# A new order for the first two fifths of a one-core adaLN, linear-attention and gated-MLP kernel

## The chip, the cores and the metric

The kernel runs on one core of a Trainium2 chip. The core has five engines that run side by side: TensorE (PE in the profile, with its weight loads as PEld), VectorE (DVE), ScalarE (ACT), GpSimd (POOL) and SyncE (SP), which here issues nearly all DMAs. Each engine works through its own list of instructions in order; semaphores hold an instruction until what it needs is there. The metric is the device time of one launch in microseconds, as the median of several runs.

## The reference

All data is bfloat16. `x` has 2048 rows of 512, there are 32 heads of 16, and the MLP has 1376 hidden columns.

```
mod = (silu(c) @ w_mod) as six rows sa, ca, ga, sb, cb, gb of 512
h   = layernorm(x) * (1 + ca) + sa
q, k, v = split(h @ wqkv)                      # 32 heads of 16
pq, pk  = q @ w_phi, k @ w_phi                 # per head, 16 x 16
phi_q   = concat(softmax(pq), softmax(-pq));  phi_k likewise
kv, z   = sum over s of phi_k (x) v,  sum over s of phi_k
o   = (phi_q @ kv) / (phi_q @ z + 1e-6)
x   = x + ga * (o @ wo)
h   = layernorm(x) * (1 + cb) + sb
x   = x + gb * ((sigmoid(h @ w_gate) * (h @ w_up)) @ w_down)
```

## The kernel before

The 2048 rows are 16 tiles of 128, called t0 to t15. The kernel is one flat program of 1230 tasks. A function builds each task with a name, the engines that may run it, what it reads and writes, and the buffers that it uses. The text `ORDER` at the head of the file then lists all task names once. `Graph.arrange` reads it from left to right: the position in the text sets the order of the tasks on each engine, and also which buffer slot a task's result gets, since slots are handed out in this order from a queue of free ones. A name without a suffix runs on the first engine in its list; `@A`, `@D` or `@P` put it on ACT, DVE or POOL. There are eight PSUM banks, seven slots of 2 KB for exponentials and features, and a few small ones. Nothing else orders the work; the kernel's estimates of task lengths are not used when it runs.

The tasks that matter here, in the order in which one tile passes through them:

- `ld_...` on SP: loads. `ld_x0b` brings tiles 2 and 3, `ld_wk0` a half of the key weights, `ld_wm00a` to `ld_wm01b` quarters of the modulation weights for the first norm.
- `warm0` (six matmuls) and `warm1_0` to `warm1_11` (one matmul each) on PE compute nothing that is used. They multiply zeros so that TensorE's clock comes up and stays up.
- `st1_t` (DVE, lines 702 and 703): mean and variance of tile t. `rs1_g` (ACT lines 709 and 710, or POOL lines 712 and 713): the reciprocal root for a group g of one or two tiles. Groups 0 and 1 are tiles 0 and 1, group 2 is tiles 2 and 3, and so on. `nmr1_g` (DVE, line 718): minus mean times this root. `xn1_t` (POOL line 731, ACT line 727; DVE line 729 for tile 0): the normalized tile.
- `tphgj` (PE, line 744): transposes of column block j of a group. For groups 6 and 7 a DMA does it (`xT1_t`, line 736). `hm1_gj` (DVE, ACT or POOL, lines 751 and 753): scale and shift by the modulation, into `h1T`.
- `modc1.0` and `modc1.1` (PE, line 630) with `modc1c0` and `modc1c1` make the modulation for column blocks 0 and 1, and for 2 and 3.
- `tpwk`, `wTck`, `fold1j`, `foldc1j` (PE and ACT in turn, lines 661, 664, 679, 685): `w_phi` is multiplied into the key weights, so that keys come out as `pk`. `fold0j` does it for the queries. `bd` (POOL, line 580) arranges `w_phi` as a block matrix for it.
- `Kt` (`Kta`, `Ktb` where split), `Vt`, `Qt` (PE, lines 817, 821, 871): the projections. `et` (ACT, line 776): exponentials of plus and minus `pk`. `nt` (DVE, line 780): their sums per head. `rt` (DVE line 798, or ACT lines 794 and 795): the reciprocals. `phit` (DVE or POOL, line 787): the key features. `vat` (ACT, line 836): the values with a column of ones, which `pmem` (POOL, lines 586 and 587) has written. `kvt` (PE, line 282): the sums over rows, into two PSUM banks. A number behind a dot says which eighth of the heads a split task begins with.
- `qet`, `qnt`, `qphit.s` (ACT line 776, DVE line 780, POOL or DVE line 784): the same for queries. `pTt` (SP): a DMA transposes the query features.
- `kvz0`, `kvn0`, `kvz1`, `kvn1` (DVE, lines 299 and 294) copy the finished sums out, and `num0a` (PE, line 326) is the first numerator. Then come `rd`, `u`, `oT`, `out`, `x1`, the second norm (`st2`, `rs2`, `nmr2`, `xn2`), and the MLP (`g`, `tg`, `u`, `hm`, `y`, `fin`).

Of the kernel before, what the change touches and what calls it, by code (L numbers as in the profile page):

```python
# [1058 lines left out]
```

## Time and profile before

| what | us |
|---|---|
| runs shown | 202.90, 204.34, 409.55 |
| their median | 204.34 |
| the profiled execution, its own time | 203.25 |
| its span, from the first to the last instruction | 201.3 |
| first numerator on PE | 56.47 |

The third run took twice as long as the others and is not used. In the rows of the profile the first two numbers are the start and the length in microseconds; a number in square brackets is the idle time of the engine before the row, with what ended it. An instruction's row often reaches about 0.1 us over the start of the next one on its engine, so what an instruction costs is best read from start to start. A row with x2 or more merges neighbours of one line and form. Row lengths of PE include the time that a result takes to come out; the pace of a row of matmuls is the distance of their starts.

### The profile page before, as it was taken

To read this page: it belongs to the slowest core of one execution; us is meant where nothing else is said; L and a number is where in the kernel's file an instruction comes from. 1 tells how busy PE (TensorE), PEld (TensorE's weight loads), DVE (VectorE), ACT (ScalarE), POOL (GpSimd) and SP (SyncE) were. 2 spreads that over 40 slices of the span, in tenths; PEclk is the share of its full clock that TensorE was granted. 3 is DMA by queue.
4 is the path that set the end of the run, shared out by engine and by line. 5 is a ranking of instruction groups with operands and counts; after the bars stand their busy time and mean duration, and the time that the engine had idled before them with its cause. 6 is when DMAs were issued, how large, how long until landed. Compare 5 with 4: busy or idle time off the path is not lost.

```text
span 201.3 us, 4128 instructions
## 1 busy us (share of the span) xinstructions
PE 193.6 (96%) x1447; PEld 106.1 (53%) x1471; DVE 160.0 (79%) x376; ACT 104.9 (52%) x250; POOL 103.9 (52%) x146
## 2 busy tenths in 40 slices
PE   7889999999999999999999999999999999999993
PEld 2555665455565777668744444444444444444442
DVE  3999999999999999997997796875969662326632
ACT  2899999999978974486621215312112420334100
POOL 4889978887899998876660166130030332000000
PEclk9999999999999999999999999999999999999999
DMA  5999956729964883455573334442113031000011
GB/s 163 336 292 236 295 204 126 113 62 268 396 248 78 133 111 68 85 34 105 104 80 80 70 62 102 84 110 56 25 25 74 2 78 55 26 8 26 28 55 55
DMA packets 49453, 22.94 MB, mean 114 GB/s; under 512 B 38065, under 2 KB 47634, under 8 KB 49426
## 3 DMA queue, kind: packets, MB, share of 16 engines
q1 hardware_dynamic: 48896, 22.59, 48.8%
q8 instruction: 13, 0.21, 0.4%
q14 instruction: 14, 0.11, 0.2%
q10 hardware_dynamic: 530, 0.02, 0.1%
HBM read 11.58 MB, written 2.10 MB: 68 GB/s over the span
## 4 chain that ended last, share of the span: by engine, by line
PE 64%; DVE 26%; issue 5%; ACT 2%; DMA 1%; DVEq 0%
PE y_ps L485 19%; PE u_ps L447 18%; PE g_ps L447 18%; DVE ks L780 6%; PE a_ps L356 5%; DVE st L702 5%; DVE qks L780 3%; DVE phi L787 3%; DVE kr L798 2%; PE num L326 2%; DVE h1T L753 2%; DMA x_sb<-in_A_x_dram 1%; DVE mv L703 1%; PE g_ps L449 1%; DVE nmr L718 1%
## 5 line engine op out<-in xcount | busy, mean ns | idle before, releaser
L457 ACT ACTIVATE tg<-g_ps 128x512 bf16<-128x512 f32 (+5 forms) x66 | 28.7, 455 | 66.6 <-PE g_ps L447 39.7
L468 DVE SCALAR_TENSOR_TENSOR wmod_sb<-tg,u_ps 128x512 bf16<-128x512 bf16 (+4 forms) x63 | 30.2, 491 | 18.1 <-ACT tg L457 11.5
L485 PE MATMUL y_ps<-wd_sb,wmod_sb 128*128 128x512 bf16 (+4 forms) x180 | 44.2, 366 | 0.2
L447 PEld LDWEIGHTS <-wg_sb 128*128 128x128 bf16 (+1 forms) x252 | 21.9, 99 | 16.1 <-issue 0.2
L447 PEld LDWEIGHTS <-wu_sb 128*128 128x128 bf16 (+1 forms) x252 | 21.7, 99 | 15.9 <-issue 0.2
L784 POOL TENSOR_TENSOR qphi<-qe,qks 128x512 bf16<-128x512 bf16 x24 | 25.2, 1066 | 3.9 <-DMA pT<-qphi 1.6
L485 PEld LDWEIGHTS <-wmod_sb 128*128 128x128 bf16 (+1 forms) x187 | 17.1, 98 | 16.0 <-issue 0.6
L447 PE MATMUL u_ps<-wT_sb,wu_sb 128*128 128x512 bf16 (+2 forms) x124 | 23.8, 322 | 0.1
L447 PE MATMUL g_ps<-wT_sb,wg_sb 128*128 128x512 bf16 (+2 forms) x122 | 23.0, 321 | 0.2
L447 PE MATMUL g_ps<-wqk_sb,wg_sb 128*128 128x128 bf16 (+4 forms) x127 | 19.9, 286 | 0.1
L447 PE MATMUL u_ps<-wqk_sb,wu_sb 128*128 128x128 bf16 (+4 forms) x127 | 19.8, 286 | 0.1
L492 DVE TENSOR_TENSOR ot<-y_ps,x 128x512 bf16<-128x512 f32 (+2 forms) x17 | 11.1, 654 | 10.4 <-PE y_ps L485 10.3
L780 DVE TENSOR_REDUCE ks<-e 128x64 f32<-128x1024 bf16 (+2 forms) x22 | 19.2, 901 | 0.0
L780 DVE TENSOR_REDUCE qks<-qe 128x64 bf16<-128x1024 bf16 x16 | 19.1, 1202 | 0.0
L376 POOL TENSOR_SCALAR ve<-mv 128x2 f32<-128x2 f32 (+1 forms) x8 | 1.8, 225 | 33.3 <-DVE mv L366 33.2
L776 ACT ACTIVATE e<-k_ps 128x512 bf16<-128x512 f32 (+2 forms) x44 | 18.2, 519 | 0.0
L776 ACT ACTIVATE qe<-q_ps 128x512 bf16<-128x512 f32 x32 | 17.0, 611 | 0.8 <-POOL phi L787 0.5
L817 PE MATMUL k_ps<-wqk_f,h1T 128*128 128x512 bf16 x61 | 16.0, 379 | 0.1
L787 POOL TENSOR_TENSOR phi<-e,kr 128x1024 bf16<-128x1024 bf16 (+2 forms) x10 | 14.8, 1484 | 2.6 <-DVE phi L787 1.2
L356 PE MATMUL a_ps<-wo_sb,oT 128*128 128x512 bf16 x60 | 15.9, 379 | 0.2
L871 PE MATMUL q_ps<-wqk_f,h1T 128*128 128x512 bf16 x61 | 15.7, 379 | 0.1
L821 PE MATMUL v_ps<-wv_sb,h1T 128*128 128x512 bf16 x61 | 15.4, 379 | 0.1
(132 smaller groups left out, 305.6 us busy)
## 6 DMA issues: line engine op xcount, KB each, us to landing
out_dram<-ot SPq DMA_DIRECT2D x15, 128.0 KB, 1.7
x_sb<-in_A_x_dram SPq DMA_DIRECT2D x6, 256.0 KB, 4.7
wmod_sb<-in_w_mod_dram SPq DMA_DIRECT2D x1, 1536.0 KB, 7.0
wu_sb<-in_B_w_up_dram SPq DMA_DIRECT2D x1, 1376.0 KB, 11.5
wg_sb<-in_B_w_gate_dram SPq DMA_DIRECT2D x1, 1376.0 KB, 11.9
wd_sb<-in_B_w_down_dram SPq DMA_DIRECT2D x1, 1280.0 KB, 8.5
wmod_sb<-in_w_mod_dram SPq DMA_DIRECT2D x4, 256.0 KB, 6.1
wqk_sb<-in_A_wqkv_dram SPq DMA_DIRECT2D x2, 256.0 KB, 4.4
```

The lines of the kernel that those rows point to most:

```text
L356: pe.matmul(ap_[:], lhsT=oT[:, j, :], rhs=wo_sb[:, j, :], start=(j == 0), stop=(j == KT - 1))
L447: pe.matmul(ps[:fsz, 0:n], lhsT=w[:, j, ft * P:ft * P + fsz], rhs=h[:, j, 0:n], start=(j == 0), stop=(j == KT - 1))
L457: G.add(f"tg{k}.{ft}", {"ACT": 0.13 + n * 0.00083}, lambda e, tg=tg, g_ps=g_ps, fsz=fsz, n=n: act.activation(tg[:fsz, 0:n], g_ps[:fsz, 0:n ...
L468: dve.scalar_tensor_tensor(hm_all[:fsz, hm[k].slot, ft, 0:n], tg[:fsz, 0:n], 1.0, u_ps[:fsz, 0:n], op0=ALU.add, op1=ALU.mult)
L485: mm = pe.matmul(y[:, 0:c1 - c0], lhsT=hm_all[:fsz, hm[k].slot, ft, tl * P:(tl + 1) * P], rhs=wd_sb[:fsz, ft, c0:c1], start=(ft == 0), sto ...
L776: act.activation(ee[:, a:b, s].rearrange("p g f h -> p g (f h)"), kp[:, a * 64:b * 64].rearrange("p (g n) -> p g n", n=64), ACT.Exp, scale ...
L780: dve.tensor_reduce(ks[:, a:b].rearrange("p g s h -> p (g s) h"), ee[:, a:b].rearrange("p g s f h -> p (g s) h f"), axis=AX.X, op=ALU.add)
L784: engine(e).tensor_tensor(ph[:].rearrange("p (g s f h) -> p g s f h", s=2, f=DH, h=4)[:, :, s], ee[:, :, s], ks[:, :, 1 - s].unsqueeze(2). ...
L787: engine(e).tensor_tensor(ph[:, a * P:b * P].rearrange("p (g f h) -> p g f h", f=DH, h=4), ee[:, a:b].rearrange("p g s f h -> p (g s) f h" ...
L817: pe.matmul(kp[:], lhsT=h1T[:, j, t * P:(t + 1) * P], rhs=wqk_f[:, j, D:2 * D], start=(j == 0), stop=(j == KT - 1))
L821: pe.matmul(vp[:], lhsT=h1T[:, j, t * P:(t + 1) * P], rhs=wv_sb[:, j, :], start=(j == 0), stop=(j == KT - 1))
L871: pe.matmul(qp[:], lhsT=h1T[:, j, t * P:(t + 1) * P], rhs=wqk_f[:, j, 0:D], start=(j == 0), stop=(j == KT - 1))
```

## The change

The first 405 names of `ORDER`, up to the copies of `wo` before the first numerators, stand in a new order. From there on the text is the same. Three tasks change engine: `xn1_3` from ACT to POOL, `rs1_0` from POOL to ACT, and `qphi2.0` from DVE to POOL. Besides this,

- on PE, five warm-ups instead of eight stand ahead of the first transposes of the key weights (`tpw1`, `tpw0`), and the others are spread out; tile 1 goes ahead of tiles 3, 0 and 2 in the key projections;
- on POOL, `pmem` moves from ahead of `bd` to behind `xn1_3` and `xn1_2`;
- on DVE, the statistics and the scale-and-shift tasks change places, `hm1_10` comes after `nmr1_4` and `st1_11` instead of before, and the sums of the keys run in the order 3, 0, 1, 2 instead of 0, 2, 3, 1;
- on ACT, `foldc13` comes ahead of the `hm1` tasks, and the exponentials run in the order 1, 3, 0, 2 instead of 0, 2, 3, 1;
- on SP, only `wmod_free`, which issues nothing, changes places with `ld_wu0`.

Which slot of a bank or buffer a task gets follows the new text too.

```diff
--- before.py
+++ after.py
@@ -37,25 +37,25 @@
 SPLIT = {"wk": 2, "wv": 1, "wq": 2, "wg": 1, "wu": 1, "x1": 2, "x2": 2, "x3": 1}
 LETTER = {"A": "ACT", "D": "DVE", "P": "POOL"}
 ORDER = """
-wdz warm0 c1 warm1_0 warm1_1 warm1_2 warm1_3 warm1_4 warm1_5 warm1_6 warm1_7 ld_x0b pmem ld_x0a ld_wk0 tpw1 tpw0 bd c2 mask4 st1_3 st1_2 st1_1 ld_x1b warm1_8
-rs1_2 rs1_1 nmr1_2 ld_wk1 xn1_3@A c3 wTc1 ld_x1a warm1_9 xn1_2 tph22 tph20 tpw2 tph21 wTc0 nmr1_1 st1_6 wTc2 xn1_1 tph13 ld_wm00b st1_0 tph10 tpw3 wTc3 fold10
-rs1_0@P fold12 st1_7 foldc10 ld_wm00a foldc12 fold11 modc1.0 rs1_4@P ld_x2b warm1_10 foldc11 modc1c0 st1_5 tph11 tph12 ld_wm01b warm1_11 st1_4 rs1_3@P
-hm1_20@A xn1_0 hm1_10 hm1_11@A hm1_21@A tph01 tph23 fold13 tph00 nmr1_4 xn1_6 xn1_7 ld_wm01a st1_11 hm1_01@A foldc13 st1_10 modc1.1 K3a modc1c1@D ld_x2a
-hm1_00@A tph02 hm1_23 rs1_6@P hm1_13@A hm1_02 nmr1_3 st1_9 st1_8 xn1_5 tph03 K0a tph41 hm1_03@A tph40 xn1_4 K2a hm1_22@A hm1_12@A hm1_41@A hm1_40 wqT1 nmr1_6
-ld_x3a st1_15 fold01 foldc01 tph42 K2b hm1_42@A K0b K3b e0.0 ld_wv0 tph32 tph30 tph31 wqT3 tph33 rs1_5@P nmr1_5 K1a hm1_32 xn1_11 hm1_30@A st1_14 n0.0 st1_12
-xn1_10 xn1_9 K1b e2.0 e3.0 rs1_8@P V0a wqT2 xn1_8 hm1_31@A tph43 V2a V2b nmr1_8 xn1_15 xn1_14 ld_wmga wqT0 V3a V3b va3 V0b fold03 V1a modca.0 modca.1 hm1_33
-tph50 V1b e1.0 K5a n2.0 r0.0@A modcac hm1_50 n3.0 hm1_43@A foldc03 xT1_11 fold02 fold00 foldc02 phi0.0 tph52 foldc00 xT1_10 va2 va1 n1.0 va0 K5b K4a r3.0
-st1_13 tph53 hm1_63@P hm1_60@P K4b hm1_62@P Q0 hm1_53@A tph51 Q1 ld_wmm2 tph82 hm1_51@A r2.0@A Q2 r1.0 phi3.0@D phi1.0@D hm1_82@A qe0.0 Q4 modc2.0 phi2.0@D
-rs1_7@P nmr1_7 xn1_12 hm1_52 qe2.0 ld_wo xn1_13 kv0.0 kv1.0 kv2.0 tph83 kv3.0 qe1.0 qn0.0 xT1_12 e5.0 modc2.1 xT1_13 modc2c K6a K6b qphi0.0@P e4.0 qn2.0
-qphi0.1@P tph80 qn1.0 pT0 hm1_80@A qphi2.1 qphi2.0 pT2 K7a K7b qe4.0 n4.0 V6 va6 r4.0@A n5.0 V5 va5 tph81 V4 qn4.0 phi4.0@D qphi1.1@P r5.0@A va4 qphi1.0@P
-hm1_70@P K9 K8 hm1_61@P qphi4.0@P kv4.0 pT1 phi5.0 hm1_72@P qphi4.1 e6.0 hm1_83 hm1_81 V9 n6.0 V7 pT4 hm1_71 e9.0 e7.0 va7 K11 n9.0 e8.0 e11.6 e11.0 r6.0
-r9.0@A ld_wd2 n7.0 kv5.0 r7.0@A e11.2 gwa K14 V8 e14.0 phi6.0 e14.4 e11.4 n8.0 n11.6 phi7.0@D n11.0 K10 n14.0 n11.2 r8.0 r11.0 va9 kv6.0 hm1_73@P e10.0 gra
-va8 K12 phi9.0 kv7.0 K15 n11.4 r11.2 V10 phi8.0 V11 n14.4 r14.0 r11.6 gwb e12.0 va10 K13 kv8.0 phi11.6 kv9.0 Q6 ld_wd r11.4 n10.0 r14.4@A wmod_free V14 V13
-phi11.4@D va11 n12.0 r10.0@A phi11.0@D phi11.2@D e13.4 phi10.0@D e13.0 e15.4 kv10.0 e15.0 kv11.4 kv11.6 ld_wu0 kv11.0 kv11.2 n13.4 va13 grb V12 Q3 wo1 phi14.0
-r12.0@A phi14.4 V15 qe6.0 va12 n13.0 r13.4 phi13.4 n15.0 r13.0 n15.4 r15.4@A phi15.4 r15.0 va14 phi13.0@D phi15.0@D Q5 phi12.0@D ld_wg0 kv12.0 kv13.0 va15
-kv14.0 qn6.0 wo0 wo3 kv15.0 kvz0 kvn0 kv13.4 kv14.4 kv15.4 kvz1 kvn1 num0a num1a num2a wo2 rd0a wo_all rd1a qe3.0 u0a num0b num4a num1b rd0b Q11 qe5.0 rd2a
-u0b u2a rd4a num2b qn3.0 u1a rd1b tpo0 Q8 qphi6.0@P qphi6.1@P oT0 out0 num4b rd2b u1b wd0 qe11.0 u2b qphi3.1@P qphi3.0@P x1_0 rd4b st2_0 qe8.0 Q7 qe7.0 tpo1
-oT1 Q10 Q9 out1 Q15 oT2 rs2_0 qn5.0 nmr2_0 xn2_0 u4a u4b x1_1 qn7.0 tsw xnT0 out2 qphi5.1@P qphi5.0@P pT6 mod02 mod00 qphi7.0@P pT3 mod03@A mod01@A qe15.0
+ld_x0b wdz warm0 c1 bd mask4 c2 ld_x0a ld_wk0 warm1_0 st1_3 warm1_1 warm1_2 st1_2 warm1_3 warm1_4 rs1_2 tpw1 st1_1 rs1_1 tpw0 ld_x1b nmr1_2 ld_wk1 wTc1
+warm1_5 warm1_6 fold11 wTc0 st1_0 rs1_0 warm1_7 tpw3 xn1_3 xn1_2 tph22 ld_x1a fold10 c3 nmr1_1 st1_7 pmem st1_6 tph21 st1_5 tpw2 warm1_8 foldc11 wTc3 ld_wm00b
+ld_wm00a xn1_1 tph10 wTc2 tph11 fold13 ld_x2b st1_4 warm1_9 fold12 foldc10 modc1.0 xn1_0 ld_wm01b foldc13 rs1_4@P nmr1_4 warm1_10 ld_wm01a warm1_11 foldc12
+tph23 rs1_3@P tph00 xn1_7 modc1c0 hm1_11@A tph02 tph01 hm1_00@A st1_11 tph20 tph13 hm1_10 hm1_01@A tph12 hm1_21@A st1_10 modc1.1 modc1c1@D ld_x2a nmr1_3
+hm1_20@A xn1_6 wqT1 K1a hm1_12@A rs1_6@P tph03 hm1_02 K3a hm1_03@A hm1_23 hm1_22@A tph41 xn1_5 st1_8 fold01 hm1_13@A tph43 hm1_43@A hm1_41@A K2a foldc01 st1_9
+tph40 K2b xn1_4 K1b nmr1_6 K0a ld_x3a hm1_40 tph30 rs1_5@P tph32 tph33 tph31 e1.0 st1_15 hm1_33 ld_wv0 K3b xn1_10 K0b V1a V1b st1_14 st1_13 hm1_30@A wqT3 e3.0
+nmr1_5 xn1_11 rs1_8@P n3.0 V3a wqT2 nmr1_8 ld_wmga hm1_31@A V0a V3b V0b fold03 e0.0 V2a modca.0 e2.0 wqT0 xn1_9 xn1_8 va1 va3 modca.1 xn1_15 n0.0 modcac
+r0.0@A hm1_32 tph50 hm1_50 V2b K4a va0 va2 xT1_11 n1.0 xn1_14 phi0.0 xT1_10 hm1_63@P tph52 hm1_60@P tph53 fold00 ld_wmm2 hm1_62@P r3.0 tph80 r1.0 K4b n2.0
+hm1_53@A K5a st1_12 phi1.0@D tph51 K5b foldc03 phi3.0@D fold02 rs1_7@P foldc00 ld_wo V5 foldc02 hm1_51@A tph42 hm1_61@P Q0 hm1_80@A r2.0@A phi2.0@D Q2
+hm1_42@A qe0.0 nmr1_7 Q1 hm1_52 kv0.0 kv1.0 qe2.0 va5 qe1.0 qn0.0 xn1_12 xT1_12 tph82 qn2.0 kv2.0 kv3.0 xn1_13 K6a K6b modc2.0 xT1_13 hm1_82@A tph83 qphi0.0@P
+modc2.1 e4.0 qphi0.1@P qn1.0 qphi2.1 pT0 e5.0 qphi2.0@P Q4 V6 n4.0 V4 qe4.0 K7a n5.0 hm1_70@P r4.0@A K7b qn4.0 phi4.0@D modc2c va4 tph81 qphi1.1@P va6 V7
+qphi1.0@P K9 pT2 qphi4.0@P r5.0@A e6.0 va7 qphi4.1 hm1_83 kv4.0 V10 e9.0 K8 K10 e7.0 pT1 pT4 phi5.0 n6.0 K11 kv5.0 hm1_71 e8.0 hm1_81 r6.0 n9.0 V8 r9.0@A
+e11.6 n7.0 r7.0@A e11.4 V9 hm1_72@P phi6.0 e11.2 ld_wd2 e11.0 hm1_73@P n8.0 n11.6 phi7.0@D r8.0 kv6.0 gwa n11.0 n11.4 n11.2 r11.0 r11.4 K14 va9 gra phi9.0
+kv7.0 va8 gwb e14.0 r11.2 r11.6 e14.4 n14.4 n14.0 e10.0 n10.0 K12 e12.0 va10 V12 va12 K15 r14.0 ld_wd phi8.0 K13 phi11.0@D phi11.6 r10.0@A n12.0 r14.4@A kv8.0
+e13.4 e13.0 kv9.0 Q5 V11 phi11.2@D phi10.0@D ld_wu0 wmod_free Q6 phi11.4@D kv10.0 va11 wo1 phi14.0 kv11.4 n13.4 kv11.0 n13.0 r13.4 e15.0 n15.0 e15.4 kv11.2
+r12.0@A phi14.4 kv11.6 n15.4 r13.0 V15 V13 phi13.4 V14 qe6.0 va13 r15.4@A Q3 r15.0 phi15.4 phi13.0@D phi15.0@D va14 phi12.0@D kv12.0 kv13.4 qn6.0 grb kv13.0
+va15 wo3 kv14.0 kv15.0 kvz0 kv14.4 ld_wg0 kvn0 kv15.4 wo0 kvz1 kvn1 num0a num1a num2a wo2 rd0a wo_all rd1a qe3.0 u0a num0b num4a num1b rd0b Q11 qe5.0 rd2a u0b
+u2a rd4a num2b qn3.0 u1a rd1b tpo0 Q8 qphi6.0@P qphi6.1@P oT0 out0 num4b rd2b u1b wd0 qe11.0 u2b qphi3.1@P qphi3.0@P x1_0 rd4b st2_0 qe8.0 Q7 qe7.0 tpo1 oT1
+Q10 Q9 out1 Q15 oT2 rs2_0 qn5.0 nmr2_0 xn2_0 u4a u4b x1_1 qn7.0 tsw xnT0 out2 qphi5.1@P qphi5.0@P pT6 mod02 mod00 qphi7.0@P pT3 mod03@A mod01@A qe15.0
 qphi7.1@P Q13 g0.8 x1_2 tg0.8 g0.1 st2_1 wd1 rs2_1 tg0.1 u0.8 u0.1 g0.0 num3b g0.4 hm0.1 hm0.8 pT5 qe9.0 tg0.4 g0.9 wd2 u0.4 u0.9 rd3b u3b tg0.9 g0.5 num3a
 hm0.4 hm0.9 u0.2 u0.0 num6a tg0.5 tg0.0 rd3a u3a u0.5 g0.2 hm0.0 hm0.5 rd6a nmr2_1 qe10.0 tg0.2 oT4 g0.10 u0.10 wd6 hm0.2 g0.3 pT7 tg0.3 u6a g0.6 num6b u0.3
 y0.0 y0.1 rd6b tg0.10 hm0.10 hm0.3 num5a num5b u6b rd5b wd3 wd4 wd5 oT3 oT6 xn2_1 qe13.0 tg0.6 rd5a y0.2 u5b g0.7 tg0.7 out4 u5a oT5 qn11.0 u0.6 u0.7 xnT1
```

## The prediction

> **What bounds the kernel now.** I read the page's busy times first, then the busy time by stretches, then the chain of waits.
>
> ```profile
> PE 193.6 (96%) x1447; PEld 106.1 (53%) x1471; DVE 160.0 (79%) x376; ACT 104.9 (52%) x250; POOL 103.9 (52%) x146
> ```
>
> The page puts PE at 96%, but that hides stages. The stretches below have, in columns, PE, PEld, DVE, ACT and POOL busy, then clock, DMA share and GB/s. I cut them at the first x tile (3.60), the first key exponential (16.27), the moved `qphi2.0` (32.38), the first `kvz` (55.92) and the point where the chain goes over to PE (67.76).
>
> ```profile
> 3.60:16.27 12.67, 11.47 (x118) 6.67 (x119) 12.15 (x42) 10.73 (x29) 9.86 (x17) 1.00 1.12 309
> 16.27:32.38 16.11, 15.95 (x182) 9.99 (x184) 15.97 (x34) 16.05 (x41) 14.62 (x20) 1.00 0.95 221
> 32.38:55.92 23.54, 23.24 (x187) 11.96 (x189) 23.50 (x44) 22.56 (x68) 19.62 (x18) 1.00 0.75 205
> 55.92:67.76 11.84, 11.32 (x102) 6.41 (x101) 11.81 (x33) 10.40 (x22) 11.68 (x12) 1.00 0.52 142
> 67.76:201.30 133.54, 129.26 (x862) 70.35 (x876) 96.00 (x227) 43.84 (x96) 45.85 (x63) 1.00 0.34 64
> ```
>
> DVE is idle for 0.52, 0.14, 0.04 and 0.03 us in the first four, 0.73 us in 64. ACT is as full from 16.27 on. So the stage that the change reorders is held by DVE, with ACT beside it. An order can win there the idle 0.73 us and what it takes off DVE, no more, unless instructions themselves get shorter. The chain says what carries a gain to the end:
>
> ```profile
> 60.91 0.68 DVE x L361
> 62.60 0.96 issue
> 63.80 0.81 ACT xn L400
> 64.63 1.28 ACT L387
> ...
> 67.76 0.38 PE u_ps L447 x4
> ...
> 192.81 5.02 PE y_ps L485 x33
> ```
>
> DVE's `x1_0` starts the first norm of the second half, the table load follows on ACT, and from 67.76 the end is PE's work in a row. The text of the order is the same from `kv15.4` and `wo0` on, so every tenth by which DVE reaches the numerators earlier should arrive at the end, and no more than that.
>
> **The change, part by part.** Three tasks change engine, the rest is permuted.
>
> *`qphi2.0` from DVE to POOL.* First DVE's rows, then POOL's.
>
> ```profile
> 32.05 0.75 DVE L784 TENSOR_TENSOR qphi<-qe,qks 128x512 bf16<-128x512 bf16 x2
> 32.72 2.33 DVE L780 TENSOR_REDUCE ks<-e 128x64 f32<-128x1024 bf16 x2
> ...
> 28.48 1.52 POOL L731 TENSOR_SCALAR xn<-x_sb,rs,nmr 128x512 bf16<-128x512 bf16 x2 [0.94 <-DVE nmr L718]
> 30.02 2.07 POOL L784 TENSOR_TENSOR qphi<-qe,qks 128x512 bf16<-128x512 bf16 x2
> 32.94 2.07 POOL L784 TENSOR_TENSOR qphi<-qe,qks 128x512 bf16<-128x512 bf16 x2 [0.85 <-ACT h1T L751]
> ...
> 36.88 1.27 POOL L784 TENSOR_TENSOR qphi<-qe,qks 128x512 bf16<-128x512 bf16 x1 [0.79 <-DVE phi L787]
> ```
>
> Two `qphi` hold DVE from 32.05 to 32.72, so one is worth 0.335 us: DVE **-0.34**. POOL pays 2.07/2 = 1.04. It has 0.94 + 0.85 + 0.79 = 2.58 us of waits around that place, and the new order moves `hm1_61` into the first of them and `qphi2.0` before `hm1_70`, into the second. Cover gone, `qphi4.0` and `phi5.0` would come 1.04 later; DVE has nothing to do with them, `kv5.0` would. The transposes `pT2` and `pT1` queue behind it on SP; the numerators read them, which stand behind `kvz1` (below). So I take 0 for POOL.
>
> A row here speaks against more POOL work: the `qphi4.0` at 36.88, beside DVE's two-input `phi4.0`, took 1.27 where its like took 1.04. [...]
>
> *`xn1_3` from ACT to POOL, `rs1_0` from POOL to ACT, `pmem` behind them.*
>
> ```profile
> 6.13 0.29 ACT L709 ACTIVATE ve<-mv,eps 128x1 f32<-128x1 f32 x1 [0.20 <-DVE mv L703]
> ...
> 6.57 0.80 ACT L727 ACTIVATE xn<-x_sb,nmr,rs 128x512 bf16<-128x512 bf16 x1
> 7.27 2.03 ACT L664 COPY wT_sb<-tp_w 128x512 bf16<-128x512 bf16 x4
> 9.17 1.59 ACT L685 CAST wqk_f<-fold_ps 128x512 bf16<-128x512 f32 x3
> ...
> 2.47 0.64 POOL L586 MEMSET vaug<- 128x32 bf16 x4
> ...
> 6.35 1.52 POOL L731 TENSOR_SCALAR xn<-x_sb,rs,nmr 128x512 bf16<-128x512 bf16 x2
> 8.61 0.24 POOL L712 TENSOR_SCALAR ve<-mv 128x1 f32<-128x1 f32 x1 [0.74 <-DVE mv L703]
> ...
> 10.99 0.28 POOL L712 TENSOR_SCALAR ve<-mv 128x2 f32<-128x2 f32 x1 [0.46 <-DVE mv L703]
> ```
>
> ACT gives up the stretch 6.57 to 7.27 (0.70) and takes over an `rs1` pair, 6.13 to 6.57 (0.44): **-0.26**. POOL adds one `xn` (0.76) and the memsets (0.64) behind `bd`, and drops `rs1_0` (8.61 up to `rs1_4`, some 0.9): +0.5 against waits of 0.74 + 0.46, so `rs1_3`, which waits for DVE's statistics at 10.99, starts there as before. Tiles 2 and 3 are then normalized at 6.35 + 1.52 = 7.87, half a microsecond later, and tile 1 at about 9.3. On PE `tph22`, `fold10`, `tph21` and `tpw2` queue behind that wait; `tpw2` would end near 9.1, while ACT packed end to end wants it for `wTc2` at 6.57 + 2 x 0.48 + 0.44 + 0.50 + 0.48 = 8.95. That costs ACT 0 to 0.2.
>
> *Where ACT's gain goes.* The second half of the modulation waits for a load whose place in SP's queue is unchanged:
>
> ```profile
> 12.58 0.55 PE L630 MATMUL modc_ps<-sc_bf,wmod_sb 128*128 128x1 bf16 x16 [0.46 <-DMA wmod_sb<-in_w_mod_dram]
> ...
> 13.23 0.13 DVE L638 TENSOR_TENSOR modc<-modc_ps,mone 128x4 f32<-128x4 f32 x1
> ...
> 13.39 0.46 ACT L751 ACTIVATE h1T<-tp_h,modc 128x128 bf16<-128x128 bf16 x1
> ```
>
> Before, ACT comes to `hm1_13` at 13.39, just as `modc1c1` ends at 13.36, with all four `foldc1` and `hm1_20`, `21`, `11`, `00`, `01` behind it. In the new order exactly the same tasks stand before `hm1_12`, the first that needs `modc1c1`. ACT gets there at 13.13 and waits until 13.4. So ACT's 0.26 is lost, and equally hides the 0.2 above: ACT **0**. From there to `e1.0` its list has the same lengths as that to `e0.0`.
>
> DVE's list between 3.60 and `modc1c1` holds the same tasks, so it gets there at the same time: 0. The new starts of the key features (`n3.0` after `st1_13`, tile 1 ahead of tile 0 on PE) only permute. `xT1_11` leaves behind `xn1_10` now, one `xn` (0.76) later, and `ld_wmm2` and `ld_wo` behind it on SP; their readers, `modc2.0` and `wo1`, come far behind the first exponentials: 0. `pmem` is read by the `va` copies, and they too come behind these. `wmod_free`, which changes place with `ld_wu0` on SP, is an empty task.
>
> *The end of the stage.* Does DVE's 0.34 get through?
>
> ```profile
> 54.07 0.23 ACT L795 ACTIVATE kr<-ks 128x32 bf16<-128x32 f32 x1
> ...
> 54.38 1.40 POOL L787 TENSOR_TENSOR phi<-e,kr 128x512 bf16<-128x512 bf16 x1 [0.72 <-ACT kr L795]
> ...
> 54.93 1.21 PE L282 MATMUL kvacc<-vaug,phi 128*128 128x68 bf16 x32
> ...
> 56.34 0.21 DVE L299 SCALAR_TENSOR_TENSOR kvb<-kvacc,mask 128x16 bf16<-128x16 f32 x1
> ```
>
> ACT's `r15.4` lets POOL's `phi15.4` run to 55.78, PE's last `kv15.4` ends at 56.14, and DVE's `kvz1` starts at 56.34. `r15.4` has the same tasks ahead of it on ACT as before, so this branch stays where it is, and `kvz1` can move by 56.34 - 56.14 = 0.20 less one hand-over, not by 0.34. Ends of this term: 0.34 and 0; I take **-0.15**, nearest to the last row.
>
> Sum against the profiled execution: 203.25 (span 201.3, and 1.95 around it) - 0.15 = **203.1 us**. The other two usable runs were 202.90 and 204.34; the median shown, 204.34, lies 1.1 above the profiled execution, and I forecast for an execution like the profiled one.
>
> **The rivals.** The warm-up of TensorE decides both of the first two.
>
> ```profile
> 1.25 2.74 PE L600 MATMUL warm<-wd_sb 128*128 128x512 bf16 x6 [1.25 <-DVE wd_sb L593]
> ...
> 4.11 2.15 PE L600 MATMUL warm<-wd_sb 128*128 128x512 bf16 x8
> ...
> L600 PE MATMUL warm<-wd_sb x18: 376/380/634, 1.2 to 11.0; 128*128 128x512 bf16 x18
> ...
> 6.09 0.61 PE L661 MATMUL tp_w<-ident,wqk_sb 128*128 128x128 bf16 x8
> 6.54 0.59 PE L600 MATMUL warm<-wd_sb 128*128 128x512 bf16 x2
> ...
> 10.67 0.16 ACT L635 COPY modc<-modc_ps 128x2 f32<-128x2 f32 x1
> ...
> 11.12 0.34 DVE L753 TENSOR_SCALAR h1T<-tp_h,modc 128x128 bf16<-128x128 bf16 x1
> ```
>
> Six warm-ups take 2.74 with 0.63 for the last: (2.74 - 0.63)/5 = 0.42 apart. The two at 6.54 are 0.59 - 0.38 = 0.21 apart. The eight at 4.11 would take 7 x 0.21 + 0.38 = 1.85 at that pace and took 2.15, so the pace doubled within the first two, near 4.7. Narrow transposes are (0.61 - 0.22)/7 = 0.055 apart, 0.11 at half pace.
>
> *A, the clock often rises later.* Let it rise at 8.0. Before: eight warm-ups last to 4.11 + 3.36 = 7.47, `tpw1` is there at 8.1 instead of ACT's 7.27; the second `tpw` (to 8.25), two warm-ups, two `tph` and `tpw2` follow (0.42 + 0.22 + 0.22 + 0.2 of drain), to 9.3, where ACT packed wants `wTc2` at 7.27 + 2 x 0.48 = 8.23. So ACT is 1.1 late, `modc1c0` (10.67) goes to 11.8, and `hm1_10` on DVE, which starts 0.2 behind it at 11.12, waits about 0.9. That makes 203.25 + 0.9 = 204.2. After: five warm-ups end at 6.21, `tpw1` is ready at 6.85, `tpw2` near 9.5 against 8.95, the gate at 13.4 swallows half of it, and `hm1_10` stands behind `nmr1_4` and `st1_11`, 1.0 later, and does not wait. That gives 203.1 to 203.4, **203.3**, a gain of 0.9 on such a run. For it: the runs differ by 1.4. Against: no second course is seen. [...]
>
> *B, slower: the thinner warm-up delays the rise.* With five instead of eight warm-ups ahead of `tpw1`, PE rests from about 5.5 to 6.1, and again before `fold11` and `tph22`. If that keeps it at half pace until 11, the queue runs: 6.21, two `tpw` 7.09, two warm-ups 7.93, `fold11` 8.37, warm-up 8.79, `tpw3` 9.23, `tph22`, `fold10`, `tph21`, `tpw2` 10.55, ready 10.75 against 8.95: ACT 1.8 late, 1.5 behind the gate, and DVE follows its exponentials: 203.25 + 1.5 = **204.8**. It decides when the pace still is 0.42 at `tpw1`. Against: here the pace had doubled by 4.7, when both orders are alike but for three warm-ups. For 2% it would have to last into the key projections.
>
> *C, the ends lock.* A bank or a hand-over in the new order costs DVE what it won, or POOL is late with `phi15.4`: 203.25 + 0.2 to 0.6, **203.7**. For it: ACT and DVE have next to no slack. Against: all counted queues come out at or under the old times.
>
> **How the numbers follow.** Forecast (203.1) 0.5, A 0.25, B 0.1, C 0.15. The low end is the lowest run shown less DVE's idle time and the moved task: 202.9 - 0.73 - 0.34 = 201.8. The high end is B with half of the 1.1 by which the median lies above the profiled execution: 204.8 + 0.4 = 205.2. A difference of 2%, 4.1 us, is about what a measurement of this kernel can tell from no change. Faster by that is four times what DVE's rows can give: 0.02. Slower needs B twice over: 0.05. Within: 0.93.
>
> **What would show it.** DVE busy in the first four stretches should fall by 0.3, POOL's rise by 1; `modc1c1` should stand at 13.2 and ACT should idle 0.2 just after it; the first exponential should start at 16.3; `qphi2.0` should appear among POOL's rows near 32, without a wait at `qphi4.0`; `kvz1` should start near 56.2 after a gap of 0.2; PE should take over near 67.6. Wrong would be DVE gaps above 0.5 us anywhere between 4 and 56, a `tpw2` after 9.5, or a pace of 0.42 after 6 us. A start of `kvz1` before 56.0 would say that ACT's branch moved too, and the gain be larger.

## The result and the profile after

The changed kernel takes 204.93 us (median of 21 runs, 203.99 to 207.38), the kernel before 203.72 beside it (21 runs). The ratio is 1.006, with a 95% interval from 1.0037 to 1.0083: 0.6% **slower**, about 1.2 us, where 0.15 us of gain was forecast. Ratios here leave out runs over 1.5% above the fastest of their kernel, so they need not equal the ratio of the medians that stand beside them. The profiled execution of the changed kernel took 205.03 us, with a span of 203.2.

Its page and its stretches, cut at the same times as those of the kernel before (columns: PE, PEld, DVE, ACT, POOL busy, clock, DMA share, GB/s):

```profile
PE 194.7 (96%) x1447; PEld 105.8 (52%) x1471; DVE 161.6 (80%) x375; ACT 104.9 (52%) x251; POOL 104.2 (51%) x146
```

```profile
3.60:16.27 12.67, 11.78 (x116) 6.41 (x118) 11.85 (x40) 10.16 (x29) 9.85 (x20) 1.00 1.16 299
16.27:32.38 16.11, 16.00 (x182) 9.93 (x183) 15.97 (x33) 15.99 (x38) 15.35 (x22) 1.00 0.98 224
32.38:55.92 23.54, 22.25 (x158) 11.07 (x159) 22.97 (x42) 21.69 (x66) 18.71 (x17) 1.00 0.86 192
55.92:67.76 11.84, 10.96 (x113) 6.24 (x113) 11.75 (x32) 9.92 (x21) 11.06 (x11) 1.00 0.50 158
```

The third stretch tells most. DVE, idle there for 0.04 us before, is now idle for 23.54 - 22.97 = 0.57, and PE and ACT are busy for about a microsecond less. DVE's busy time on the page rose by 1.6 us although it has one instruction less: some of its instructions became longer. The chain of waits through that stretch names the place:

```profile
37.98 0.03 POOLq L787
38.01 0.33 POOL qphi L784
38.35 0.02 issue
38.36 4.61 DMA pT<-qphi
...
43.06 0.45 ACT e L776 x2
...
43.74 0.27 ACT kr L795
...
44.02 0.04 DVE phi L787
44.06 1.46 issue
45.51 0.54 DVE kr L798
```

ACT's exponential `e11.6` waits for a DMA, the transpose `pT4` of query features, with which its arithmetic has nothing to do. Timelines of ACT, DVE and POOL of the changed kernel at that place (start, length; in brackets the idle time and what ended it):

```profile
43.06 0.45 ACT L776 ACTIVATE e<-k_ps 128x128 bf16<-128x128 f32 x2 [1.05 <-DMA pT<-qphi]
...
43.53 0.42 DVE L780 TENSOR_REDUCE ks<-e 128x16 f32<-128x256 bf16 x1 [0.43 <-ACT e L776]
44.02 1.57 DVE L787 TENSOR_TENSOR phi<-e,kr 128x1024 bf16<-128x1024 bf16 x1
45.51 0.54 DVE L798 RECIPROCAL kr<-ks 128x64 bf16<-128x64 f32 x1
...
43.14 1.90 POOL L787 TENSOR_TENSOR phi<-e,kr 128x1024 bf16<-128x1024 bf16 x1
```

The same task `phi7.0` in the kernel before, at the same place of DVE's list, with no wait in front of it:

```profile
43.03 0.73 DVE L787 TENSOR_TENSOR phi<-e,kr 128x1024 bf16<-128x1024 bf16 x1
43.69 1.33 DVE L780 TENSOR_REDUCE ks<-e 128x16 f32<-128x256 bf16 x3
```

Three things are to be seen. ACT stands for 1.05 us. DVE's sum `n11.6` follows `e11.6` and waits 0.43. Then `phi7.0` keeps DVE from 44.02 to 45.51 instead of from 43.03 to 43.69, 0.83 longer, while POOL's `phi9.0` runs from 43.14 to 45.04. Following DVE's tasks by their starts, the changed kernel is 0.30 behind at `n8.0` (41.89 for 41.59), which stands just ahead of this place, and 2.07 behind at `n13.4` (52.50 for 50.43); 0.43 + 0.83 = 1.26 of these 1.77 lie in the rows above. `kvz0` starts at 57.93 instead of 55.92, and the lag stays to the end.

Why `e11.6` waits for `pT4` is read from the text and not from the trace. The seven 2 KB slots are dealt out in the order of the text, so a task waits for the last reader of the slot that it is dealt. Before, `e11.6` got the slot of `qe4.0`, which `qphi4.1` had read last, and `e14.0`, at 42.90, got the one that `pT4` had read (issued at 38.18, landed at 41.43). In the new text the deal has moved by one at this point: `e11.6` gets the slot that `pT4` read last, and the transpose took 4.61 us from issue to landing.

### The profile page after: what moved, and what is told of

It reads as the page before. It is cut to its first block, busy times and chain, and to the rows that moved or that the text cites. A ratio compares the mean times of both kernels' runs of the same rounds, so it can differ in the third digit from the quotient of the medians.

```text
span 203.2 us, 4133 instructions
## 1 busy us (share of the span) xinstructions
PE 194.7 (96%) x1447; PEld 105.8 (52%) x1471; DVE 161.6 (80%) x375; ACT 104.9 (52%) x251; POOL 104.2 (51%) x146
## 4 chain that ended last, share of the span: by engine, by line
PE 77%; DVE 7%; DMA 5%; issue 4%; SPq 3%; ACT 2%; POOL 0%; ACTq 0%; POOLq 0%; DVEq 0%
PE y_ps L485 19%; PE u_ps L447 18%; PE g_ps L447 17%; PE a_ps L356 5%; PE k_ps L817 4%; PE v_ps L821 3%; DMA wmod_sb<-in_w_mod_dram 3%; PE q_ps L871 3%; DMA pT<-qphi 2%; PE num L326 2%; DVE ks L780 2%; SPq L537 1%; PE g_ps L449 1%; DVE qks L780 1%; DVE phi L787 1%
## 5 line engine op out<-in xcount | busy, mean ns | idle before, releaser
L784 POOL TENSOR_TENSOR qphi<-qe,qks 128x512 bf16<-128x512 bf16 x25 | 26.3, 1070 | 2.9 <-DMA pT<-qphi 1.4
```

Of the source, the lines that this page charges most:

```text
L784: engine(e).tensor_tensor(ph[:].rearrange("p (g s f h) -> p g s f h", s=2, f=DH, h=4)[:, :, s], ee[:, :, s], ks[:, :, 1 - s].unsqueeze(2). ...
```

## The experiments

Three theories went in. **Theory 1**: the slot of `pT4` under `e11.6` is the loss; with 1a, that its price comes by pushing `phi7.0` under POOL's `phi9.0`, and 1b, that ACT's late exponentials cost by themselves. **Theory 2**: the new early order (warm-ups, statistics, first exponentials) is the loss. **Theory 3**: `qphi2.0` on POOL is the loss. Every kernel below computes the whole reference. Diffs are of the text of the order, with the names broken into lines.

**pT4 later in the text.** Each engine's list stays as it is in the changed kernel; only the slots are dealt differently, and `e11.6` gets the one that `phi5.0` read last.

```diff
 e7.0 pT1
-pT4
 phi5.0 n6.0
...
 phi6.0 e11.2
+pT4
 ld_wd2
```

> The changed kernel, with the word pT4 moved in the order's text to just before ld_wd2. Every engine's list stays that of the changed kernel; only the buffer slots are dealt differently: e11.6 on ACT gets the slot that POOL's phi5.0 leaves (40.2 us in the profile of after) instead of the one that the transpose pT4 leaves (landed at 42.97), and phi9.0 gets that one. Theory 1 (the loss comes from ACT waiting for pT4's slot): the idle of 1.05 before e11.6 goes, DVE's phi7.0 no longer falls under POOL's phi9.0, and the median falls from 204.9 by 1.0 to 1.5, to 203.4 to 203.9. Theory 2 (the new start of the kernel loses: thinner warm-up, xn1_3 on POOL) and theory 3 (qphi2.0 on POOL delays the transposes): no change, 204.7 to 205.1.

Measured: 203.53 us (203.38 to 203.89), ratio to the kernel before 0.9991 (0.996 to 1.0021). ACT in its profile, with no wait in front, and DVE's `phi7.0`, short again:

```profile
41.56 0.43 ACT L776 ACTIVATE e<-k_ps 128x128 bf16<-128x128 f32 x2
...
43.52 0.69 DVE L787 TENSOR_TENSOR phi<-e,kr 128x1024 bf16<-128x1024 bf16 x1 [0.44 <-POOL phi L787]
```

Moving a name that changes no engine's list takes 1.4 us off. Three more tasks are dealt another slot by it (`phi6.0`, `phi7.0` and `phi9.0`), but none of these waits in the profile of the changed kernel. Theory 1 holds.

**`qphi2.0` back on DVE**, the rest as changed.

```diff
-qphi2.0@P
+qphi2.0
```

> The changed kernel, with qphi2.0 back on DVE; all else as in the change. Theory 1: pT4 is issued when qphi4.0 ends on POOL, which waits for DVE's phi4.0 and not for qphi2.0, so e11.6 still waits for its landing; DVE has 0.34 more to do: 204.9 to 205.3. Theory 3: pT2 and pT1 leave 1 us earlier, pT4 lands earlier, and the median falls to about 203.7. Theory 2: 204.9 to 205.3.

Measured: 205.06 us, ratio 1.007 (1.004 to 1.0099). ACT still waits 0.92 at `e11.6`, and `phi7.0` takes 1.93. Theory 3 falls as the cause of the loss.

**The early half alone**, and **the late half alone**. The first has the tasks that the kernel before lists up to `qe0.0` in the changed order, then the rest as before; the second the other way round. In the first, `e11.6` gets the slot of `qe4.0` as before; in the second, that of `pT4`.

The seams, the early half against the changed kernel and the late half against the kernel before:

```diff
-hm1_42@A qe0.0 nmr1_7 Q1 hm1_52 kv0.0 kv1.0 qe2.0 va5 qe1.0 qn0.0
+hm1_42@A qe0.0 Q1 tph82 hm1_82@A Q4 modc2.0 phi2.0@D rs1_7@P nmr1_7
...
-hm1_82@A qe0.0 Q4 modc2.0 phi2.0@D rs1_7@P nmr1_7 xn1_12
+hm1_82@A qe0.0 tph80 rs1_7@P ld_wo V5 hm1_61@P hm1_80@A phi2.0@D
...
```

> Early half of the change alone: the tasks that the kernel before has up to qe0.0 (27 us) stand in the changed order, with xn1_3 and rs1_0 on their new engines, and all later ones as before, qphi2.0 on DVE. e11.6 gets the slot that qphi4.0 and qphi4.1 leave, as before. Theory 1 and theory 3: 203.3 to 203.9, like before. Theory 2: all of the loss, 204.7 to 205.1.

> Late half of the change alone: up to qe0.0 the order of before, then the changed order, with qphi2.0 on POOL. e11.6 gets pT4's slot as in the change. Theory 1 and theory 3: all of the loss, 204.6 to 205.2. Theory 2: 203.3 to 203.9, like before.

Measured: early half 203.50 us, ratio 1.0001 (0.9969 to 1.0033); late half 205.86 us, 1.0122 (1.0073 to 1.0172). Theory 2 falls: the early order by itself costs and wins nothing that can be told, and the loss comes with the late one. The late half alone even loses about twice what the whole change does (with intervals that overlap): `phi7.0` is 0.80 longer in it than in the changed kernel, and the rest was not followed up. ACT, DVE and POOL of the late half show the same picture as the changed kernel:

```profile
42.80 0.45 ACT L776 ACTIVATE e<-k_ps 128x128 bf16<-128x128 f32 x2 [0.42 <-DMA pT<-qphi]
...
44.02 2.37 DVE L787 TENSOR_TENSOR phi<-e,kr 128x1024 bf16<-128x1024 bf16 x1
...
43.94 1.91 POOL L787 TENSOR_TENSOR phi<-e,kr 128x1024 bf16<-128x1024 bf16 x1
```

**The slot put into the kernel before.** Two names move ahead of `e11.6`, so that it is dealt `pT4`'s slot; every engine's list is that of the kernel before.

```diff
 n9.0 e8.0
+r6.0 phi6.0
 e11.6 e11.0
-r6.0
 r9.0@A
...
 e14.0
-phi6.0
 e14.4
```

> The kernel before, with the words r6.0 and phi6.0 moved in the order's text to just ahead of e11.6. All five engines' lists stay those of the kernel before; phi6.0 now takes the slot that e11.6 had, and e11.6 takes the one that the transpose pT4 leaves, as in the change. Theory 1 (that slot is enough to lose the time): ACT's e11.6, at 41.03 in the profile of before, waits for pT4's landing (41.43 there), so for 0.4 to 1.5, DVE's phi7.0 comes under POOL's phi9.0 (at 43.54 there) in some runs and then lasts until 0.55 behind its end: 203.5 to 205.0, about 1 above before, with an idle before e11.6 in the profile. If the order of the engines is what loses: 203.0 to 204.0, as before.

Measured: 205.12 us, but from 202.96 to 207.24, ratio 1.0012 (0.9968 to 1.0056). The profiled execution has the wait (0.64 at `e11.6`) and a `phi7.0` of 2.39 us. Its executions reach from near the lowest of the kernel before (202.78 beside it) to beyond the highest of theory 1, and the interval holds both no loss and half of it. Of the eight with a mean granted clock of 0.996 or more, five took 202.96 to 204.01 and three 205.73 to 206.22, and the kernel before took at most 205.10 beside them with such a clock. That fits a loss that comes in some executions only, as was expected, but none of these eight was profiled. So that the same slot is all it takes in the other text too stays undecided.

**`phi7.0` three sums later**, in the changed kernel, so that DVE reaches it after POOL's `phi9.0`. This tells 1a from 1b: by 1a most of the 0.83 that `phi7.0` was longer should come off the 204.93, for a time near 204.1; by 1b the time stays.

```diff
 n8.0 n11.6
-phi7.0@D
 r8.0 kv6.0 gwa n11.0 n11.4 n11.2
+phi7.0@D
 r11.0
```

> The changed kernel, with DVE's phi7.0 moved behind n11.0, n11.4 and n11.2 (about 1 us of DVE's work), so that POOL's phi9.0 is through when it starts. e11.6 keeps pT4's slot and its wait. [...] Theory 1b (ACT's wait itself is the loss, the long phi7.0 only fills time in which DVE would wait for ACT): phi7.0 is short again, DVE idles instead, and the median stays at 204.6 to 205.1.

Measured: 205.80 us, ratio 1.01 (1.0048 to 1.0153). Three of its six executions had a mean granted clock of 0.99 (the last section is on these) and took 206.37 to 206.53; the other three took 204.72 to 205.23, about where 1b put them. DVE of this kernel:

```profile
42.89 0.42 DVE L780 TENSOR_REDUCE ks<-e 128x16 f32<-128x256 bf16 x1 [0.25 <-ACT e L776]
43.22 0.54 DVE L798 RECIPROCAL kr<-ks 128x64 bf16<-128x64 f32 x1
44.38 1.07 DVE L780 TENSOR_REDUCE ks<-e 128x16 f32<-128x256 bf16 x3 [0.61 <-ACT e L776]
45.37 0.68 DVE L787 TENSOR_TENSOR phi<-e,kr 128x1024 bf16<-128x1024 bf16 x1
```

`phi7.0` is 0.68 long again, as wanted, but DVE now stands 0.25 + 0.61 for ACT's exponentials. The collision is not the loss by itself: take it away and DVE waits for ACT instead. 1a falls, 1b stays.

**`qphi2.0` to POOL in two other surroundings**: with the early half (so all three changes of engine, without the late order), and in the kernel before as its only change.

```diff
-qphi2.0
+qphi2.0@P
```

> The early half of the change (as in the run of the early half alone) with qphi2.0 on POOL, the rest as before: all three engine changes without the changed late order. The prediction's term: 0.15 to 0.34 below the early half alone (203.50), so 203.15 to 203.4. If POOL's later qphi2.0 holds up pT2, whose slot qphi4.0 takes here, POOL idles before qphi4.0 and phi5.0 and phi6.0 come late: 203.5 to 204.2.

> The kernel before with the one engine change qphi2.0 from DVE to POOL. The prediction's term: 0.15 to 0.34 below before. If pT2's slot holds up POOL's qphi4.0: 0 to 0.7 above before.

Measured: 205.10 us, ratio 1.0062 (1.0029 to 1.0095), against 203.50 for the early half alone; and 204.88 us, ratio 1.0042 (1.0 to 1.0085). So the move that was to win 0.34 on DVE costs in the first, by more than either of the two ranges allowed; in the second the interval just reaches no change. DVE of the kernel before with this one move, and a row of POOL near 55:

```profile
33.08 2.35 DVE L780 TENSOR_REDUCE ks<-e 128x64 f32<-128x1024 bf16 x2 [0.23 <-ACT e L776]
...
37.10 0.69 DVE L784 TENSOR_TENSOR qphi<-qe,qks 128x512 bf16<-128x512 bf16 x1
...
54.36 2.25 DVE L787 TENSOR_TENSOR phi<-e,kr 128x512 bf16<-128x512 bf16 x3
...
54.99 1.07 POOL L787 TENSOR_TENSOR phi<-e,kr 128x512 bf16<-128x512 bf16 x1 [0.45 <-ACT kr L795]
```

Of the 0.34, 0.23 goes at once: `n4.0` comes to DVE before ACT has `e4.0`. Then DVE's two-input instructions fall under POOL's, since all of DVE is shifted and POOL's list is longer: `qphi4.1` takes 0.69, where 0.42 was its length in the same place before (POOL's `hm1_61`, under way when it starts, ends at 37.52), and the three `phi` at the end take 2.25 and end at 56.61, 0.55 after POOL's `phi15.4` (56.06). In the early half with the move, `qphi4.1` takes 1.27 and the three `phi` 2.24. In the changed kernel the same move makes no difference that can be told (205.06 without it, 204.93 with it): what it costs depends on what it pushes together.

**Better than both?** Three more kernels on top of the first one: `qphi2.0` back on DVE; `n11.4` ahead of `phi7.0`, where DVE had 0.44 to spare; and both.

```diff
-qphi2.0@P
+qphi2.0
...
 n8.0 n11.6
+n11.4
 phi7.0@D r8.0 kv6.0 gwa n11.0
-n11.4
 n11.2
```

> The changed kernel with pT4 later in the text, and qphi2.0 back on DVE. Theory 1b (what holds the stage is ACT and DVE together, so a task less on POOL helps only where it takes a collision of two-input operations off DVE): with pT4 late there are few such collisions left, so 203.2 to 203.6 against 203.53 with pT4 late alone. Rival (the moved qphi2.0 always costs what it cost the kernel before, 0.7): 202.8. Rival (it is worth the 0.34 that the prediction gave it on DVE): 203.9.

> The changed kernel with pT4 later in the text, and n11.4 ahead of phi7.0 on DVE. With pT4 late, DVE waits 0.44 ahead of phi7.0, until POOL's phi6.0 ends; n11.4 is 0.28 long and its exponential is there by 42.76. If DVE alone holds the stage from there, it wins 0.28: 203.25. If ACT's exponentials or PE hold it too, DVE waits at the next sums instead and the time stays at 203.5.

> pT4 late, n11.4 ahead of phi7.0, qphi2.0 on DVE. If the two small gains add: 203.0, which would be under the kernel before. If the stage is locked between ACT and DVE: 203.4 to 203.6, level with the kernel before.

Measured: 203.83 us, ratio 1.0021 (0.9992 to 1.005); 204.07, 1.0019 (0.9986 to 1.0053); 203.78, 1.0013 (0.9987 to 1.0038). None is told from the kernel before, and none from the first one. All three lie above what was expected by theory 1b or of a locked stage, and 203.83 lies next to the 203.9 of the rival by which the move wins 0.34 on DVE. Whether it wins that once the slot is out of the way stays open: putting `qphi2.0` back adds 0.30 to the first kernel and takes 0.29 off the second. The second shows how the stage is locked; DVE first, then ACT:

```profile
43.55 0.69 DVE L787 TENSOR_TENSOR phi<-e,kr 128x1024 bf16<-128x1024 bf16 x1
...
46.15 1.28 DVE L780 TENSOR_REDUCE ks<-e 128x32 f32<-128x512 bf16 x2 [0.35 <-ACT e L776]
...
44.90 2.19 ACT L776 ACTIVATE e<-k_ps 128x256 bf16<-128x256 f32 x6 [0.46 <-PE k_ps L817]
```

DVE's gap ahead of `phi7.0` shrank from 0.44 to 0.11, and 2.6 us later it waits 0.35 at `n14.4`, for an exponential that waited 0.46 for PE's projection. What DVE wins there, it hands back.

| kernel | us | ratio to before |
|---|---|---|
| changed | 204.93 | 1.006 |
| changed, `pT4` later in the text | 203.53 | 0.9991 |
| changed, `qphi2.0` on DVE | 205.06 | 1.007 |
| early half | 203.50 | 1.0001 |
| late half | 205.86 | 1.0122 |
| before, with the slot of `pT4` under `e11.6` | 205.12 | 1.0012 |
| changed, `phi7.0` later | 205.80 | 1.01 |
| early half and `qphi2.0` on POOL | 205.10 | 1.0062 |
| before and `qphi2.0` on POOL | 204.88 | 1.0042 |
| `pT4` later, `qphi2.0` on DVE | 203.83 | 1.0021 |
| `pT4` later, `n11.4` earlier | 204.07 | 1.0019 |
| all three | 203.78 | 1.0013 |

## Why the prediction was wrong

The time, 204.93, lies inside the range, but on the other side of no change.

**The step that failed** is the argument against rival C, "all counted queues come out at or under the old times". It counted the queues of the engines and of SP and left out the queue of slots, so the sum has no term for a slot that comes free late. Where the prediction did look at the transposes, in the part on `qphi2.0`, the gap shows: "The transposes `pT2` and `pT1` queue behind it on SP; the numerators read them, which stand behind `kvz1` (below). So I take 0 for POOL." It asked who reads a transpose's result, and not who is dealt the buffer that the transpose frees. The kernel's own rule, that slots follow the text, was known and was not worked through, although a new order of 405 names moves many deals. What the runs showed in its place: `e11.6` is dealt `pT4`'s slot, waits 1.05 for it, and the kernel loses the 1.4 us that come back when `pT4` moves in the text. The move of `qphi2.0` is not what did it: with that task back on DVE the wait is still 0.92.

**The gain of 0.15** from `qphi2.0` is the second step that did not hold. DVE did get its 0.34: with the first exponential 0.45 late (16.72 for 16.27), `n4.0` is only 0.11 late (32.83 for 32.72). But the sentence that "every tenth by which DVE reaches the numerators earlier should arrive at the end" took DVE's 0.14 and 0.04 us of idle time to mean that what DVE wins there arrives, though the prediction had just put ACT beside it. In the experiments DVE then waits 0.23 at `n4.0` for ACT, and 0.35 at `n14.4` for an exponential that waited for PE. As the only change this move cost 0.4% (an interval that reaches down to 1.0), in the early half 0.6%; with `pT4` late its sign is open.

**A row pointed there and was priced on the wrong engine.** The prediction took POOL's `qphi4.0` of 1.27 for 1.04 as a cost to POOL. (It named `phi4.0` as the instruction beside it; by the rows that had ended at 36.78, and the one beside it was `qphi4.1`, from 36.81.) In the runs the larger price is DVE's: the 0.73 of `phi7.0` became 1.57 and 2.37.

**What held.** ACT's gain is lost at the gate, as forecast: `modc1c1` runs at 13.67, and ACT waits just behind it,

```profile
13.87 2.52 ACT L751 ACTIVATE h1T<-tp_h,modc 128x128 bf16<-128x128 bf16 x6 [0.24 <-DVE modc L638]
```

0.24 for the 0.2 expected, at `hm1_12`. It stands at 13.67 and not at 13.2 since the load that it waits for came later in this execution: PE's weight loads for `modc1.1`, which a DMA holds up in both profiles, start at 13.08 instead of 12.58 (the first `x` tile was late too, with `st1_3` at 3.83 for 3.60). That the early order itself is worth nothing that can be told the early half shows, with 1.0001. `tpw2` ended at 9.15 (9.1 was forecast). POOL took `qphi2.0` in its waits, with 0.71 left in front of `qphi4.0`:

```profile
30.52 3.30 POOL L784 TENSOR_TENSOR qphi<-qe,qks 128x512 bf16<-128x512 bf16 x3
33.80 0.55 POOL L753 TENSOR_SCALAR h1T<-h1T,modc 128x256 bf16<-128x256 bf16 x1
34.32 2.07 POOL L784 TENSOR_TENSOR qphi<-qe,qks 128x512 bf16<-128x512 bf16 x2
37.11 1.23 POOL L784 TENSOR_TENSOR qphi<-qe,qks 128x512 bf16<-128x512 bf16 x1 [0.71 <-DVE phi L787]
```

`kvz1` started at 58.34 (56.2 was forecast) and PE took over at 69.86 (67.6), and the mark set for being wrong, a DVE gap above 0.5 between 4 and 56, was nearly met by the 0.43 at `n11.6`; the long `phi7.0` beside it is no gap, and the marks would have missed it. DVE's and POOL's busy time in the four stretches fell by 0.89 and 0.81, where 0.3 less and 1 more were forecast; with the lag, work had slid out of these windows, so they say nothing.

**The rivals.** C was the nearest: a hand-over in the new order costs DVE more than it won. It was priced at 0.2 to 0.6 and measured 1.2. A's second course is there. The rows of PE at the start,

```profile
4.11 2.31 PE L600 MATMUL warm<-wd_sb 128*128 128x512 bf16 x5
6.53 0.62 PE L661 MATMUL tp_w<-ident,wqk_sb 128*128 128x128 bf16 x8
```

show five warm-ups at (2.31 - 0.63)/4 = 0.42 apart throughout; the two at 6.99 take 0.60 and are 0.60 - 0.38 = 0.22 apart. The granted clock came up at 6.39, where it came up at 4.65 in the profile of before. That touches one of the signs of being wrong, a pace of 0.42 after 6 us. But a late rise costs the changed order little, as A said: with `pT4` later in the text, the profiled execution had its clock up at 6.91 and still took 203.53. A's 0.9 for the old order was not seen: with the clock up at 7.00, in the kernel before with `qphi2.0` on POOL, `hm1_10` waited 0.15. The 8.0 that A let the rise have was its author's assumption; these four profiles show 4.65 to 7.00. B, in which the thinner warm-up holds the clock down until 11, was seen in no profile.

## What to carry to other kernels

Where buffers are dealt in the order of a program's text, moving a task moves the deal for all that follow: list, for each task near the bound, who last reads the slot that it is dealt, and look first for a slot released by a DMA (here a transpose of 4.61 us, for a wait of 1.05). Two engines that are both full can be one bound: what one wins it may wait away at the other (here 0.23 of DVE's 0.34, at `n4.0`), so a task taken off one is not yet a gain while the other's list is as long as before. Where a trace shows a pair on DVE and POOL like `phi7.0` and `phi9.0` (1.57 to 2.37 for 0.68 to 0.73), place the two apart in time; in these runs the larger price came where DVE started second.

## What was not expected of the hardware

**DVE's `phi7.0` ends 0.55 us after POOL's `phi9.0`.** Where it started while POOL was in `phi9.0`, its length was what was left of POOL's instruction (1.02 in the changed kernel, 1.82 in the late half) and 0.55 more. `phi7.0` takes 0.68 to 0.73 where it does not start under `phi9.0`. Under `phi9.0` it ended at 45.59, 45.50 and 46.39 in the changed kernel, the one with `qphi2.0` on DVE and the late half, with POOL's ends at 45.04, 44.95 and 45.84: 0.55 each time, for lengths of 1.57, 1.93 and 2.37. POOL's instruction need not have two tensor inputs: in the kernel before with `qphi2.0` on POOL, the half as large `qphi4.1` of 0.69 ended 0.27 after POOL's `hm1_61`, which has one. Not every pair shows it: in the kernel before, `kvn0` and `kvn1`, two-input as well but with an f32 input by their rows, took 0.41 each (from 56.01 and 56.42) while POOL's `wo` ran from 55.74 to 56.90, and ended 0.49 and 0.07 before it. On DVE, the sum `n11.6`, which has one tensor input, took 0.42 beside the same `phi9.0`. In the pair where DVE started first, POOL paid, and less: in the kernel before `phi15.4` took 1.40 beside a DVE `phi` that was under way, and ended 0.91 after it; with `qphi2.0` moved it starts first, takes 1.07, and DVE's is the long one.

**The same transpose lands in 3.1 to 4.6 us.** For the four transposes of query features issued between 32 and 39, the median from issue to landing is 3.2 in both kernels, the longest 3.3 before and 4.6 after. The longest is `pT4`'s in the changed kernel (38.36 to 42.97). What makes it longer was not settled: it is 4.6 as well in the kernel with `pT4` later in the text.

**The clock falls again in some executions.** The profile of the kernel with the slot put into before caught it (columns as in the stretches above):

```profile
9.00:12.00 3.00, 2.62 (x34) 1.71 (x35) 2.90 (x11) 2.97 (x10) 2.28 (x6) 1.00 1.16 310
12.00:13.00 1.00, 0.76 (x23) 0.66 (x21) 0.96 (x3) 1.00 (x4) 1.00 (x2) 0.89 1.27 239
13.00:16.00 3.00, 3.00 (x17) 1.48 (x15) 2.77 (x10) 2.79 (x7) 2.87 (x6) 0.50 1.10 335
16.00:17.00 1.00, 1.00 (x10) 0.63 (x9) 0.96 (x6) 0.41 (x1) 0.84 (x3) 0.90 3.10 258
```

The granted clock is at half from 12.78 to 16.19, 3.41 us. PE had gaps just before (2.62 us busy of 3.00, then 0.76 of 1.00); whether they matter was not tried. In the executions of the kernel before that stood beside the experiments, the mean granted clock was under 0.996 in 34 of 87, and these were 1 to 3 us longer by their medians (204.72 to 206.21 for 203.15 to 203.37). Of the executions with the changed early order, the changed kernel's own among them, 14 of 111 did so; of those with the old early order and a changed late one, 10 of 30. So the new early order seems to make the fall rarer; but above 0.996 none of its kernels was faster than the kernel before (the lowest median is 203.42), and what in the order does it was not tried.
